# Keeping a weight conversion in its PSUM bank, in halves, and a last block with q in hp's bank and g rounded on ScalarE

## The chip, the cores and the metric

One Trainium2 chip, one of its cores. The metric is the device time of one execution in microseconds (us). TensorE does the matmuls, VectorE (DVE), ScalarE (ACT) and GpSimd (POOL) the elementwise work, SyncE (SP) issues the DMAs. The clock of TensorE that the profile shows as granted has two levels here, 1.2 and 2.4 GHz; a row's PEclk is its share of the higher one.

## The reference

Three layers over 3072 tokens of width 384, in float32: a linear attention with a decaying state, a layer with a curved activation, and a layer with a softmax-weighted linear unit and a normalization.

```python
for t in range(S):                      # 4 batches, 8 heads, 768 steps, head width 48
    cur = einsum('bhd,bhe->bhde', u * kt, vt)
    y[:, :, t] = einsum('bhd,bhde->bhe', rt, state + cur)
    state = wt[..., None] * state + einsum('bhd,bhe->bhde', kt, vt)
x = y as (3072, 384)
h = x @ w_in                            # 384 x 2048
x = (h - tanh(h)) @ w_out               # 2048 x 384
h = x @ w_in2                           # 384 x 1024
solu = h * softmax(h)
out = ((solu - mean) / sqrt(var + 1e-6) * g_ln) @ w_out2    # 1024 x 384
```

The weights arrive as 64-bit floats and are turned into pairs of 32-bit numbers on the chip.

## The kernel before, in words

**Stages.** The 24 units of attention (128 tokens each) feed six blocks of 512 tokens. A block has 16 steps m, one for each 128 columns of w_in. In a step `part1` makes `hp` (9 matmuls, one PSUM bank, pool `ps_h` with two buffers), then the activation is worked out in elementwise steps, and `part2`, two steps later in the program, adds 9 matmuls into the three banks `x2p`. Attention units 0 to 3 run first, the others between the steps. After the last block a second part with 24 tiles of 128 tokens does the third layer (`b_h`, `b_t`, `b_o`).

**The activation of a step** is a chain over engines: ACT squares `hp` into `t` (L339), DVE makes `y` from `hp` and `t` (L340), ACT makes a second square `p` from `t` (L342), DVE combines `p` and `y` (L344), ACT writes a range check into `q` (L345), and then `y` is rounded into `gs[:, 0]` (on ACT at L347 or on POOL at L349), and POOL writes the rest into `gs[:, 1]` (L350). In block 0 `p` is `hp` itself, in PSUM, and the rounding is on ACT; in blocks 1 to 5 `p` is `q`, in SBUF, and the rounding is on POOL.

**A conversion** (`convert`) takes 128 rows of 768 64-bit floats, half of w_in and half of w_out: `H_` are the upper words, `L_` the lower words, both with a stride of two words in the SBUF tile `raw`. ACT scales `L_` in place (L118). DVE shifts and masks `H_` into `a` (L125, the shift), joins the sign bits (L126, the or-step), and adds `L_` as an exact 32-bit integer (L127, the add; an instruction of its own that works on 16-bit elements, so 768 words are 1536 elements; the profile calls it CUSTOM_DVE_ANT_0 and the program's order ISA). Then ACT rounds into `hi` (L130) and POOL subtracts (L131).

- `conv_a` converts the first layer's weights into `wa`, 16 times, during the attention of units 0 to 3 and block 0. It passes `bank=ps_a`: `a` is a PSUM bank of the pool `ps_a`, which has three buffers and serves attention's transposes and products too.
- `conv_b` converts the second layer's weights into `wb`, 8 times, during the last block. It passes no bank, so `a` is the tile `cv_x` in SBUF, and the shift and the or-step are done in two halves of 384.

**What sets the order.** The program is recorded step by step (`fast_path`), and a scheduler then sets each engine's order. Engines run their own list in order, so an instruction that waits holds up those behind it. The tile `raw` has two buffers (pool `cvr`); the next load on SP's queue waits until the add has read `L_`.

Of the kernel before, what the change touches and what calls it, by code (L numbers as in the profile page):

```python
# [14 lines left out]
ALU = mybir.AluOpType  # L15
# [4 lines left out]
NT, DM, FF, FF2 = 3072, 384, 2048, 1024  # L20
# [5 lines left out]
NB = NT // BLK  # L26
# [29 lines left out]
class Kern:  # L56
# [52 lines left out]
    def convert(self, pool, raw, hi, lo, scale=None, bank=None):  # L109

        nc, v = self.nc, self.nc.vector
        flat = raw.rearrange("p i f two -> p (i f) two")
        H_, L_ = flat[:, :, 1], flat[:, :, 0]
        x = pool.tile([128, 2 * DM], U32, tag="cv_x", name="cv_x")
        xf = x.bitcast(F32)
        nc.scalar.activation(L_, L_, AF.Copy, scale=2.0**-29)  # L118
        for i in range(2):
            s = slice(i * DM, (i + 1) * DM)  # L120
            if bank is None:
                a = x[:, s]
            else:
                a = bank.tile([128, 4, C], F32, tag="a", name="cv_a").rearrange("p j t -> p (j t)")[:, 0:DM].bitcast(U32)
            v.tensor_scalar(a, H_[:, s], 3, 0x3FFFFFF8, ALU.logical_shift_left, ALU.bitwise_and)  # L125
            v.scalar_tensor_tensor(x[:, s], H_[:, s], 0xC0000000, a, ALU.bitwise_and, ALU.bitwise_or)  # L126
        v.tensor_tensor(x, x, L_, ALU.add)  # L127
        if scale is not None:
            nc.scalar.activation(xf[:, DM:], xf[:, DM:], AF.Copy, scale=scale)
        nc.scalar.copy(hi, xf)  # L130
        nc.gpsimd.tensor_tensor(lo, xf, hi, ALU.subtract)  # L131
# [196 lines left out]
    def part1(self, i, m):  # L328
        nc, v, g = self.nc, self.nc.vector, self.nc.gpsimd
        hp = self.ps_h.tile([128, BLK], F32, tag="h", name="hp")  # L330
        xs = self.xs[i % 2]
        seq = [(a, b, j) for j in range(KM) for a, b in ((1, 0), (0, 1), (0, 0))]
        for n, (a, b, j) in enumerate(seq):
            self.mm(hp, self.wa[:, a, m, j * 128:(j + 1) * 128], xs[:, b, j], start=n == 0, stop=n == len(seq) - 1)  # L334
        t = self.gp.tile([128, BLK], F32, tag="t", name="t")
        q = self.gp.tile([128, BLK], F32, tag="q", name="q")
        y = self.gp.tile([128, BLK], F32, tag="y", name="y")
        gs = self.gs.tile([128, 2, BLK], F32R, tag="g", name="g")
        nc.scalar.activation(t, hp, AF.Square)  # L339
        v.tensor_tensor(y, hp, t, ALU.mult)  # L340
        p = hp if i == 0 else q
        nc.scalar.activation(p, t, AF.Square, bias=self.c_fsb, scale=F_S)  # L342
        col = 2 * NU + i * NM + m
        v.scalar_tensor_tensor(y, p, F_E, y, ALU.add, ALU.mult)  # L344
        self.last_act = nc.scalar.activation(q, t, AF.Relu, bias=self.c_t2, accum_out=self.flags[:, col:col + 1])  # L345
        if i == 0:
            nc.scalar.copy(gs[:, 0], y)  # L347
        else:
            g.tensor_scalar(gs[:, 0], y, 1.0, 1.0, ALU.mult, ALU.mult)  # L349
        g.tensor_tensor(gs[:, 1], y, gs[:, 0], ALU.subtract)  # L350
        return gs
# [419 lines left out]
```

## Time and profile before

| | us |
|---|---|
| median of 3 runs | 837.1 (836.93 to 837.52) |
| the profiled execution's own time | 833.47 |
| its span, first to last instruction | 831.7 |
| PE busy in the span | 779.4 |
| DVE busy | 548.6 |
| ACT busy | 490.5 |
| POOL busy | 377.2 |

The span is what the trace covers; the execution's own time has 1.8 us around it. The busy time of PE is modelled, since matmuls are pipelined: where it is full, the interval from one matmul to the next tells more. Shares over the whole span mix stages with different limits, so they are read stage by stage.

### The profile page before, as it was taken

How to read it: one execution, taken by the hardware profiler on the slowest of the kernel's cores; microseconds unless marked ns; L12 is line 12 of the kernel's file. 1: busy time of each engine (PE TensorE's matmuls, PEld its weight loads, DVE VectorE, ACT ScalarE, POOL GpSimd, SP SyncE). 2: the span in 40 equal slices, each digit the busy share in tenths (PEclk: the TensorE clock that was granted, in tenths of full speed). 3: DMA queues.
4: the chain of work that ended last, by engine and by line, in shares of the span. 5: the costliest groups of instructions: out<-in, count | busy, mean ns of one | idle time of the engine just before them, and what ended most of it. 6: DMA issues, size and time to landing. Idle time of an engine off the chain costs nothing.

```text
span 831.7 us, 13450 instructions
## 1 busy us (share of the span) xinstructions
PE 779.4 (94%) x4706; PEld 649.1 (78%) x4706; DVE 548.6 (66%) x997; ACT 490.5 (59%) x928; POOL 377.2 (45%) x360
## 2 busy tenths in 40 slices
PE   3778988999999999999999999889989999999996
PEld 2656766778878888888888788667879999999996
DVE  4688889666664566565556763895287577667763
ACT  3436776677666767677677765655445454445442
POOL 3544765655555655556556465676412111111110
PEclk9988998899999999999999999999999999999998
DMA  9966567435455554463434220410021111111101
GB/s 164 166 107 127 138 146 151 136 100 115 90 120 114 125 108 105 107 157 81 119 100 130 82 81 25 140 50 2 10 67 39 48 39 48 39 48 39 48 29 33
DMA packets 151309, 74.32 MB, mean 89 GB/s; under 512 B 107328, under 2 KB 142784, under 8 KB 151232
## 3 DMA queue, kind: packets, MB, share of 16 engines
q1 hardware_dynamic: 151232, 73.37, 37.0%
q8 instruction: 39, 0.64, 0.3%
q14 instruction: 38, 0.31, 0.1%
HBM read 61.54 MB, written 9.44 MB: 85 GB/s over the span
## 4 chain that ended last, share of the span: by engine, by line
PE 75%; DVE 11%; DMA 4%; issue 2%; POOL 2%; ACT 2%; SPq 2%; DVEq 0%; ACTq 0%; POOLq 0%
PE hp L334 19%; PE x2p L357 18%; PE o L457 12%; PE h L412 11%; PE qk L254 3%; PE tp L218 3%; DVE cv_x L126 2%; PE tt L446 2%; DVE cv_x L127 2%; PE y L296 2%; PE y L293 2%; DMA raw<-in_moe_w_out_dram 1%; DVE cv_x L125 1%; DMA raw<-in_moe_w_in_dram 1%; PE kt L260 1%
## 5 line engine op out<-in xcount | busy, mean ns | idle before, releaser
L357 PE MATMUL x2p<-g,wa 128*128 128x512 f32 x864 | 226.4, 401 | 9.0 <-POOL g L350 4.6
L334 PE MATMUL hp<-xs,wa 128*128 128x512 f32 x864 | 225.8, 403 | 6.7 <-POOL wa L131 3.2
L334 PEld LDWEIGHTS hp<-xs,wa 128*128 128x128 f32 x864 | 162.5, 192 | 45.2 <-POOL wa L131 3.7
L357 PEld LDWEIGHTS x2p<-g,wa 128*128 128x128 f32 x864 | 160.3, 191 | 46.0 <-POOL g L350 6.3
L350 POOL TENSOR_TENSOR g<-y,g 128x512 fp32r<-128x512 f32 x96 | 129.3, 1347 | 17.4 <-ACT g L347 9.7
L340 DVE TENSOR_TENSOR y<-hp,t 128x512 f32<-128x512 f32 x96 | 66.2, 689 | 106.6 <-ACT t L339 103.6
L457 PE MATMUL o<-wb,ts 128*128 128x384 f32 x576 | 110.0, 341 | 1.0 <-DVE ts L448 1.0
L345 ACT ACTIVATE q<-t,cst 128x512 f32<-128x512 f32 x96 | 69.5, 724 | 68.1 <-DVE y L344 67.8
L412 PE MATMUL h<-wb,x2s 128*128 128x512 f32 x432 | 103.8, 392 | 2.8 <-DVE so L432 2.4
L349 POOL TENSOR_SCALAR g<-y 128x512 fp32r<-128x512 f32 x80 | 53.9, 674 | 114.8 <-DVE y L344 111.4
L457 PEld LDWEIGHTS o<-wb,ts 128*128 128x128 f32 x576 | 100.5, 188 | 2.9 <-DVE ts L448 1.3
L412 PEld LDWEIGHTS h<-wb,x2s 128*128 128x128 f32 x432 | 80.6, 188 | 19.8 <-issue 3.0
L339 ACT ACTIVATE t<-hp 128x512 f32<-128x512 f32 x96 | 56.6, 591 | 44.8 <-PE hp L334 44.6
L437 POOL TENSOR_TENSOR st<-st,cst 128x1 f32<-128x1 f32 x24 | 13.5, 563 | 136.2 <-DVE st L436 134.8
L344 DVE SCALAR_TENSOR_TENSOR y<-q,y 128x512 f32<-128x512 f32 x80 | 65.4, 818 | 10.6 <-ACT q L342 5.6
L342 ACT ACTIVATE q<-t,cst 128x512 f32<-128x512 f32 x80 | 57.7, 722 | 2.0
L435 ACT ACTIVATE e<-so 128x1024 f32<-128x1024 f32 x24 | 25.4, 1059 | 49.4 <-DVE so L434 49.4
L425 DVE TENSOR_REDUCE st<-h 128x1 f32<-128x1024 f32 x24 | 29.4, 1224 | 28.6 <-PE h L412 27.1
L428 DVE TENSOR_REDUCE part<-e 128x32 f32<-128x1024 f32 x24 | 29.3, 1220 | 27.9 <-ACT e L427 27.9
L218 PE MATMUL tp<-ident,rkw 128*128 128x128 f32 x264 | 41.9, 292 | 6.0 <-DMA rkw<-in_w_dram 5.7
L402 POOL TENSOR_TENSOR x2s<-x2s 128x384 fp32r<-128x384 f32 x24 | 24.4, 1018 | 48.3 <-ACT x2s L401 40.0
L131 POOL TENSOR_TENSOR wa<-cv_x,wa 128x768 fp32r<-128x768 f32 x16 | 29.4, 1838 | 35.3 <-ACT wa L130 35.3
(114 smaller groups left out, 1211.1 us busy)
## 6 DMA issues: line engine op xcount, KB each, us to landing
raw<-in_moe_w_out_dram SPq DMA_DIRECT2D x48, 384.0 KB, 4.0
raw<-in_moe_w_in_dram SPq DMA_DIRECT2D x64, 144.0 KB, 3.2
raw<-in_moe_w_in_dram SPq DMA_DIRECT2D x16, 384.0 KB, 3.1
rkw<-in_w_dram SPq DMA_DIRECT2D x24, 192.0 KB, 4.3
rkw<-in_r_dram SPq DMA_DIRECT2D x24, 192.0 KB, 4.5
rkw<-in_k_dram SPq DMA_DIRECT2D x24, 192.0 KB, 3.9
vt<-in_v_dram SPq DMA_DIRECT2D x24, 192.0 KB, 4.4
x2d<-x2o SPq DMA_DIRECT2D x18, 256.0 KB, 2.2
```

The lines of the kernel that those rows point to most:

```text
L218: self.nc.tensor.transpose(p[:, j], self.rkw[u % 2][:, i, 2 * j:2 * j + 2, :], self.ident)
L334: self.mm(hp, self.wa[:, a, m, j * 128:(j + 1) * 128], xs[:, b, j], start=n == 0, stop=n == len(seq) - 1)
L339: nc.scalar.activation(t, hp, AF.Square)
L340: v.tensor_tensor(y, hp, t, ALU.mult)
L342: nc.scalar.activation(p, t, AF.Square, bias=self.c_fsb, scale=F_S)
L344: v.scalar_tensor_tensor(y, p, F_E, y, ALU.add, ALU.mult)
L345: self.last_act = nc.scalar.activation(q, t, AF.Relu, bias=self.c_t2, accum_out=self.flags[:, col:col + 1])
L349: g.tensor_scalar(gs[:, 0], y, 1.0, 1.0, ALU.mult, ALU.mult)
L350: g.tensor_tensor(gs[:, 1], y, gs[:, 0], ALU.subtract)
L357: self.mm(self.x2p[d], self.wa[:, a, m, sl], gs[:, b], start=m == 0 and n == 0, stop=m == NM - 1 and n == 2)
L412: self.mm(p[:, f], xs[:, a, j], self.wb[:, b, 4 * f:4 * f + 4, j * 128:(j + 1) * 128], start=q == 0, stop=q == 8)
L457: self.mm(p, ts[:, a, k], self.wb[:, b, k, DM:], start=q == 0, stop=q == 3 * NM2 - 1)
```

## The change

In `convert` with a bank, the or-step writes back into the PSUM bank, and the add reads the bank and writes `x`, once for each half of 384 words. Without a bank (`conv_b`), the shift and the or-step are each one instruction over 768 words, in `x`, and the add stays one instruction. In the last block `p` is `hp`, and the rounding of `g` is on ACT, as in block 0.

```diff
@@ convert
-        for i in range(2):
-            s = slice(i * DM, (i + 1) * DM)
+        n = 1 if bank is None else 2
+        for i in range(n):
+            s = slice(i * 2 * DM // n, (i + 1) * 2 * DM // n)
             if bank is None:
-                a = x[:, s]
+                a = x
             else:
                 a = bank.tile([128, 4, C], F32, tag="a", name="cv_a").rearrange("p j t -> p (j t)")[:, 0:DM].bitcast(U32)
             v.tensor_scalar(a, H_[:, s], 3, 0x3FFFFFF8, ALU.logical_shift_left, ALU.bitwise_and)
-            v.scalar_tensor_tensor(x[:, s], H_[:, s], 0xC0000000, a, ALU.bitwise_and, ALU.bitwise_or)
-        v.tensor_tensor(x, x, L_, ALU.add)
+            v.scalar_tensor_tensor(a, H_[:, s], 0xC0000000, a, ALU.bitwise_and, ALU.bitwise_or)
+            v.tensor_tensor(x[:, s], a, L_[:, s], ALU.add)
@@ part1
-        p = hp if i == 0 else q
+        ends = i in (0, NB - 1)
+        p = hp if ends else q
@@
-        if i == 0:
+        if ends:
             nc.scalar.copy(gs[:, 0], y)
```

The lines of the changed kernel are numbered one higher from L120 on (the shift is L126, the or-step L127, the add L128) and two higher from L342 on (L342 is L344 there, L344 is L346, L350 is L352).

In block 0, DVE's list around the fifth conversion of `conv_a` (`cv_a` is the bank, `cv_x` the tile in SBUF, `xs` and `x` belong to attention). Before:

```order
L125 TENSOR_SCALAR cv_a<-raw 128x384
L344 SCALAR_TENSOR_TENSOR y<-hp,y 128x512
L125 TENSOR_SCALAR cv_a<-raw 128x384
L300 TENSOR_TENSOR xs_140<-y,xs_140 112x3x128
L301 TENSOR_TENSOR x_138<-y,x_138 112x128
L126 SCALAR_TENSOR_TENSOR cv_x<-raw,cv_a 128x384 x2
L125 TENSOR_SCALAR cv_a<-raw 128x384
L127 ISA cv_x<-raw,cv_x 128x1536
```

The same place in the changed kernel:

```order
L126 TENSOR_SCALAR cv_a<-raw 128x384
L301 TENSOR_TENSOR xs_140<-y,xs_140 112x3x128
L302 TENSOR_TENSOR x_138<-y,x_138 112x128
L126 TENSOR_SCALAR cv_a<-raw 128x384
L346 SCALAR_TENSOR_TENSOR y<-hp,y 128x512
L127 SCALAR_TENSOR_TENSOR cv_a<-raw,cv_a 128x384 x2
L341 TENSOR_TENSOR y<-hp,t 128x512
L128 ISA cv_x<-raw,cv_a 128x768 x2
```

The or-steps now write the bank, one add over 1536 elements has become two over 768 that read the bank, and an L341 stands between or-steps and adds, so both banks are held until after it.

At the start of the last block, DVE's list (`cv_x` and `raw` are those of `conv_b`). Before:

```order
L125 TENSOR_SCALAR cv_x<-raw 128x384 x2
L126 SCALAR_TENSOR_TENSOR cv_x<-raw,cv_x 128x384 x2
L340 TENSOR_TENSOR y<-hp,t 128x512
L127 ISA cv_x<-raw,cv_x 128x1536
L125 TENSOR_SCALAR cv_x<-raw 128x384 x2
L344 SCALAR_TENSOR_TENSOR y<-q,y 128x512
L340 TENSOR_TENSOR y<-hp,t 128x512
L126 SCALAR_TENSOR_TENSOR cv_x<-raw,cv_x 128x384 x2
L344 SCALAR_TENSOR_TENSOR y<-q,y 128x512
L127 ISA cv_x<-raw,cv_x 128x1536
```

The same place in the changed kernel:

```order
L126 TENSOR_SCALAR cv_x<-raw 128x768
L127 SCALAR_TENSOR_TENSOR cv_x<-raw,cv_x 128x768
L341 TENSOR_TENSOR y<-hp,t 128x512
L128 ISA cv_x<-raw,cv_x 128x1536
L126 TENSOR_SCALAR cv_x<-raw 128x768
L341 TENSOR_TENSOR y<-hp,t 128x512
L346 SCALAR_TENSOR_TENSOR y<-hp,y 128x512
L127 SCALAR_TENSOR_TENSOR cv_x<-raw,cv_x 128x768
L128 ISA cv_x<-raw,cv_x 128x1536
L346 SCALAR_TENSOR_TENSOR y<-hp,y 128x512
```

A conversion has three instructions in place of five, the combining step reads `hp`, and its place among the conversions hardly moves.

In the same stretch, POOL's list (`g` is `gs`). Before:

```order
L131 TENSOR_TENSOR wb<-cv_x,wb 128x768 x2
L349 TENSOR_SCALAR g<-y 128x512
L131 TENSOR_TENSOR wb<-cv_x,wb 128x768
L350 TENSOR_TENSOR g<-y,g 128x512
L349 TENSOR_SCALAR g<-y 128x512
L350 TENSOR_TENSOR g<-y,g 128x512
L131 TENSOR_TENSOR wb<-cv_x,wb 128x768
```

And in the changed kernel:

```order
L132 TENSOR_TENSOR wb<-cv_x,wb 128x768 x2
L352 TENSOR_TENSOR g<-y,g 128x512
L132 TENSOR_TENSOR wb<-cv_x,wb 128x768
L352 TENSOR_TENSOR g<-y,g 128x512
L132 TENSOR_TENSOR wb<-cv_x,wb 128x768
```

The roundings of `g` are gone from POOL; on ACT they now stand once a step, between the chain's other instructions and those of the conversions.

## Rows read from the trace of the kernel before

**Rows 1.** The page: span, busy time of each engine with its share.
```profile
span 831.7 us, 13450 instructions
PE 779.4 (94%) x4706; PEld 649.1 (78%) x4706; DVE 548.6 (66%) x997; ACT 490.5 (59%) x928; POOL 377.2 (45%) x360
```

**Rows 2.** Busy time by stretch (columns as the first line says; x counts instructions).
```profile
core 0: us, PE busy (x) PEld busy (x) DVE busy (x) ACT busy (x) POOL busy (x), PEclk, DMA share, GB/s
60.00:160.00 100.00, 87.22 (x501) 67.94 (x503) 87.52 (x152) 67.12 (x127) 59.53 (x41) 0.90 0.59 137
160.00:520.00 360.00, 359.46 (x2397) 292.80 (x2393) 215.42 (x384) 249.11 (x501) 205.59 (x196) 1.00 0.44 105
520.00:572.00 52.00, 45.03 (x180) 33.66 (x179) 44.53 (x48) 31.17 (x57) 34.20 (x27) 0.97 0.22 77
572.00:600.00 28.00, 28.00 (x125) 23.14 (x124) 10.02 (x15) 14.37 (x28) 14.29 (x15) 1.00 0.00 1
```

**Rows 3.** The chain that ended last, pieces on DVE (start us, us, what).
```profile
72.36 1.45 DVE cv_x L127
...
99.48 2.08 DVE cv_x L127
...
113.97 1.72 DVE cv_x L127
...
129.66 1.85 DVE cv_x L127
...
542.54 3.14 DVE cv_x L126 x2
```

**Rows 4.** Tile cv_x, 0 to 160 us (ns min/median/max, first and last start).
```profile
L126 DVE SCALAR_TENSOR_TENSOR cv_x<-raw,cv_a x32: 532/544/557, 16.5 to 157.6; 128x384 uint32<-128x384 uint32 x32
L127 DVE CUSTOM_DVE_ANT_0 cv_x<-raw,cv_x x16: 941/950/2143, 19.1 to 158.7; 128x1536 uint16<-128x1536 uint16 x16
```

**Rows 5.** DVE's instructions in order of time, block 0 (start us, us).
```profile
97.02 0.94 DVE L127 CUSTOM_DVE_ANT_0 cv_x<-raw,cv_x 128x1536 uint16<-128x1536 uint16 x1
97.88 0.67 DVE L344 SCALAR_TENSOR_TENSOR y<-hp,y 128x512 f32<-128x512 f32 x1
98.48 0.53 DVE L126 SCALAR_TENSOR_TENSOR cv_x<-raw,cv_a 128x384 uint32<-128x384 uint32 x1
98.94 0.54 DVE L203 TENSOR_REDUCE dg<-inv 128x8 f32<-128x384 f32 x1
```

**Rows 6.** Tile cv_x, 515 to 570 us.
```profile
L125 DVE TENSOR_SCALAR cv_x<-raw x12: 347/766/2006, 522.0 to 556.4; 128x384 uint32<-128x384 uint32 x12
L126 DVE SCALAR_TENSOR_TENSOR cv_x<-raw,cv_x x12: 545/810/2193, 524.1 to 559.3; 128x384 uint32<-128x384 uint32 x12
L127 DVE CUSTOM_DVE_ANT_0 cv_x<-raw,cv_x x6: 944/952/2389, 525.7 to 561.6; 128x1536 uint16<-128x1536 uint16 x6
```

**Rows 7.** DVE's groups, 521 to 571 us (busy us, mean ns, idle before).
```profile
L126 DVE SCALAR_TENSOR_TENSOR cv_x<-raw,cv_x 128x384 uint32<-128x384 uint32 x12 | 13.2, 1136 | 0.0
L125 DVE TENSOR_SCALAR cv_x<-raw 128x384 uint32<-128x384 uint32 x12 | 10.5, 912 | 4.0 <-POOL wb L131 4.0
L344 DVE SCALAR_TENSOR_TENSOR y<-q,y 128x512 f32<-128x512 f32 x9 | 9.5, 1053 | 1.0 <-ACT q L342 0.6
L127 DVE CUSTOM_DVE_ANT_0 cv_x<-raw,cv_x 128x1536 uint16<-128x1536 uint16 x6 | 7.1, 1190 | 0.4
L340 DVE TENSOR_TENSOR y<-hp,t 128x512 f32<-128x512 f32 x9 | 6.2, 684 | 2.9 <-ACT t L339 2.1 <-POOL g L349 0.8
```

**Rows 8.** POOL's rounding of g, 521 to 571 us.
```profile
L349 POOL TENSOR_SCALAR g<-y 128x512 fp32r<-128x512 f32 x9 | 6.8, 753 | 11.8 <-DVE y L344 11.8
```

**Rows 9.** Groups by form, whole span: block 0's forms.
```profile
L342 ACT ACTIVATE hp<-t,cst 128x512 f32<-128x512 f32 x16 | 11.0, 687 | 2.9 <-DVE y L340 2.9
L344 DVE SCALAR_TENSOR_TENSOR y<-hp,y 128x512 f32<-128x512 f32 x16 | 10.9, 683 | 1.0 <-ACT hp L342 0.9
L347 ACT CAST g<-y 128x512 fp32r<-128x512 f32 x16 | 9.8, 615 | 2.5 <-DVE y L344 2.4
```

**Rows 10.** All engines in order of time, last block.
```profile
549.49 0.69 DVE L340 TENSOR_TENSOR y<-hp,t 128x512 f32<-128x512 f32 x1 [0.69 <-ACT t L339]
...
554.25 0.68 DVE L344 SCALAR_TENSOR_TENSOR y<-q,y 128x512 f32<-128x512 f32 x1
```

**Rows 11.** What PE waited for, 60 to 165 us (us in total, times, longest).
```profile
PE hp L334 <- DVE y L344: 2.7, 1, 2.7
```

## The prediction

> **What bounds the kernel now.** The page comes first: PE is busy for 94% of the span [rows 1], which says little, since the change touches stages that differ. So the busy time by stretch comes next [rows 2]. Three kinds of stretch are to be seen. From 160 to 520 us PE is full (359.5 of 360) and DVE at 215.4 of 360, 60%: nothing that the change does to DVE, ACT or POOL is worth anything there. From 60 to 160 us (attention's first units, block 0 and the `conv_a` conversions) DVE is at 87.5% and PE is idle for 12.8 us. From 520 to 572 us (most of the last block, the `conv_b` conversions) DVE is at 44.5 of 52, 86%, and PE is not full. From 572 to 600 us the conversions are over, and PE is full again, with one matmul every 28.0 / 125 = 0.224 us.
>
> The last number says what 520 to 572 loses. Its 180 matmuls need 180 x 0.224 = 40.3 us, so 52 - 40.3 = 11.7 us are lost there, and no change to the elementwise work can win more than that in this stretch. The chain that ended last agrees on who is to blame: in both stretches it runs through the conversions on DVE [rows 3].
>
> Why do those take long? The tile's view answers. In 0 to 160 us the or-step, which reads one operand from PSUM, takes 532 to 557 ns in all 32 instances; the add, which reads both from SBUF, takes 941 ns at best and 2143 at worst [rows 4]. In the last block, where all three instructions have their operands in SBUF, all three spread: 347 to 2006, 545 to 2193, 944 to 2389 ns [rows 6]. DVE's instructions with their tensors in SBUF stretch, here beside POOL that is 60 to 66% busy [rows 2], and the ones with a PSUM operand do not.
>
> **The change, part A: `conv_a`.** The add's tail goes. Of the 16 adds five are disturbed, four of them on the chain: 1.45, 2.08, 1.72 and 1.85 us [rows 3] against 0.95, together 3.3 us too long; the fifth stands off it. Against this stand 16 more instructions. One instruction is followed by the next before its own end: an add of 0.94 us begins 0.86 us ahead of the next instruction, an or-step of 0.53 us 0.46 us ahead [rows 5]. If an add over 768 elements costs what the or-step over 384 words costs, 0.46 us (both halve 0.86 to 0.43 and pay some fixed part again), two cost 0.92 against 0.86: 16 x 0.06 = 1.0 us more. The gain on the chain is 3.3 - 1.0 = 2.3 us; I take 2.5, since POOL's own instructions are less held up too. The shift is as before. The or-step now writes PSUM, for which there is no row on DVE with PSUM on both sides. From below: the same kind of square on ACT takes 687 ns into PSUM [rows 9], and nothing on DVE suggests a gain. From above: if reading and writing took turns at the bank, each of its 384 elements would cost 1.05 ns more (0.684 us for 512 elements against 0.545 for 384 [rows 6, 7]), 0.4 us x 32 = 13 us. I take no change, being nearest to the or-step's own 545 ns [rows 4].
>
> Each bank is held through the adds instead of the or-step, about 1.5 us longer with the instructions that stand between. There are three buffers, and attention waits on DVE for longer than that anyway in this stage; I charge nothing, and 2 us if that cover is missing.
>
> **Part B: the last block.** Its 30 conversion instructions in this stretch take 13.2 + 10.5 + 7.1 = 30.8 us [rows 7]. Undisturbed they would take 12 x 0.347 + 12 x 0.545 + 6 x 0.944 = 16.4 us [rows 6]. So 14.4 us are waits, 0.48 us an instruction. Afterwards there are 18. Widths of 768 have no row. The or-step: 0.545 + 384 x 1.05 ns = 0.95 us. The shift: at 0.347 for 384 it runs at about twice that pace, so 0.347 + 0.20 = 0.55 us (at most twice 0.347, 0.69). With the add at 0.944 a conversion needs 2.45 us, six 14.7 us. The waits scale with the number of instructions and with POOL's share. POOL loses 6.8 us of rounding [rows 8]: 34.2 - 6.8 = 27.4, over a stretch of 45 us 61% against 66%. So 18 x 0.48 x 61/66 = 8.0 us. Sum 22.7 against 30.8: DVE saves 8.1 us. The combining step takes 1.053 us with its operands in SBUF [rows 7] and 0.683 with `hp` [rows 9]: 9 x 0.37 = 3.3 us. DVE falls from 44.5 to 33.1 us, below the 40.3 that PE needs.
>
> ACT takes over nine roundings of 0.615 us, and its second square becomes 0.03 us cheaper: 31.2 + 5.5 - 0.3 = 36.4 us. In a stretch of 45 us that is 81%, the highest of the elementwise engines; DVE would be at 74%. So not all of the 11.7 us comes back. For the size I use the two stretches that are known: PE loses nothing at a DVE share of 60% and 12.8% at 87.5%; in between, at 74%, 6.5% of 45 us or 3 us, and somewhat more for ACT. I take 4.7 lost and 7 us won.
>
> `hp` is held until the combining step, not just until L340. With two buffers a step may keep its bank for two steps less its own filling. At PE's pace a step is 18 matmuls, 4.0 us, so 8.1 - 2.0 = 6.0 us; t and y take 1.3 us of it, and 4.7 us are left for p and the combining step. The worst case here starts L340 at 549.49 and ends L344 at 554.93, 4.8 us after L340 [rows 10]; the usual one is far shorter. In block 0, which has this form already, PE waited on L344 once, for 2.7 us [rows 11]. So: hidden, and some 3 us if not.
>
> **The sum.** 2.5 + 7 = 9.5 us. Span 831.7 - 9.5 = 822.2; own time 833.47 - 9.5 = 824.0. The profiled execution is 3.6 us below the median of the runs shown, so the median becomes 837.1 - 9.5 = 827.6 us.
>
> **The rivals.**
>
> *The add from PSUM runs at half pace (slower).* Now 1536 elements of 16 bits pass in 0.86 us, two of them in the 1.05 ns that other instructions need for one element. If an operand in PSUM allows only one, a half of 768 elements costs some 0.46 + 384 x 1.05 ns = 0.86 us, two 1.72 instead of 0.86, and 16 x 0.86 = 13.8 us come into a stage where DVE is nearly full, less the 3.3 of the waits: +10.5. With part B at 7 us the sum is +3.5: 840.6 us. It decides from a half of (16 x 0.86 + 3.3 + 7) / 32 = 0.75 us upwards. For it: no row has a 16-bit operand in PSUM. Against it: the 32-bit instructions of DVE show no price for PSUM, 545 ns with it and 545 without [rows 4, 6]. The Trainium skill speaks on both sides. VectorE: DVE Perf Modes, section "The perf-mode tier table (the rule you actually need)", lists an operation on two tensors at its single pace as soon as any operand is in PSUM; by that rule this rival holds. Vector Engine (DVE) Microarchitecture Reference, section "Performance modes — why throughput varies by op and dtype", asks for the double pace on two sources only that all operands have 2 bytes and step one, and wants SBUF just for the mode that uses both ports on one source; by that the forecast holds. No run here shows either yet.
>
> *The last block's wait moves to `hp` and ACT.* PE waits for the combining step behind two wide conversion instructions, now up to 1 us each undisturbed, and ACT at 81% is late with p. Part B then gives back nothing: 837.1 - 2.5 = 834.6 us. For it: the combining steps of the first two steps stand behind conversion instructions in DVE's new order. Against it: [rows 11].
>
> *The wide instructions wait just as long, and the start gains nothing.* If a wait depends on the time that DVE spends in SBUF, not on the number of instructions, the 14.4 us shrink only by POOL's share, to some 13; part B is 1.7 + 1.4 + 3.3 us on DVE, worth 4, and part A is hidden behind the loads of `raw`: 833 us.
>
> **How the numbers follow.** Forecast 0.56; half pace 0.24; wait on `hp` and ACT 0.12; waits unchanged 0.08. A measurement of this kernel tells about 0.2%, 1.7 us, from no change. Faster: nearly all of the forecast (0.53), most of the second (0.09) and third rival (0.07), a little of the first (0.03), 0.72. Slower: three quarters of the first, 0.18, and 0.02 of others, 0.20. The same: 0.08. The forecast's own range is 823 (all of the 11.7 and 2.5 us) to 833; with the half pace on the other side the range is 822 to 841.
>
> **What would show it.** The add's halves at about 0.55 us each without spread mean that part A is right; 0.95 us means the first rival. The or-step into PSUM should stay at 0.55. In the last block the step interval should be near 4.1 us soon, the combining step 0.68 without spread, POOL without roundings, and PE's waits should not name L346. The prediction is wrong if the or-step in PSUM doubles, if PE waits for attention's banks in the first 160 us, or if the new order moves work in the full stretch, which should keep its 360 us.

## The result and the profile after

The changed kernel takes 823.5 us (median of 4 runs, 822.77 to 823.97) where the kernel before takes 837.3 us beside it (836.93 to 837.66): a ratio of 0.9835 with an interval of 0.9818 to 0.9852, 13.8 us less. The forecast was 827.6 us. The profiled execution of the changed kernel took 822.77 us, and its page begins so [rows 1]:

```profile
span 821.0 us, 13437 instructions
PE 769.9 (94%) x4706; PEld 643.2 (78%) x4706; DVE 528.6 (64%) x997; ACT 499.1 (61%) x944; POOL 364.9 (44%) x344
```

The two spans differ by 10.7 us (831.7 and 821.0), 3 us less than the times: the profiled execution of the kernel before, 833.47, lies below all four of its timed runs. In the later sets that kernel takes 834.4 to 834.6 us, and the two parts of the change, run alone there, win 8.5 and 2.8 us, so the size is nearer to 11 us than to 13.8. To see where these come from I set marks in both timelines: the start of the first square `t` of a step, the first reduction of the third layer, and the end. The changed kernel is ahead of the one before by:

| mark | before, us | after, us | ahead by |
|---|---|---|---|
| block 0, first step | 71.8 | 73.2 | -1.4 |
| block 1, first step | 175.1 | 165.1 | 10.0 |
| block 2, ninth step | 303.0 | 295.7 | 7.3 |
| last block, first step | 523.1 | 515.3 | 7.8 |
| last block, last step | 594.8 | 586.2 | 8.6 |
| first reduction of the third layer | 603.4 | 592.9 | 10.5 |
| end | 831.7 | 821.0 | 10.7 |

So on these two traces the start gives 7.8 us and the last block 2.7, where the prediction had 2.5 and 7. The sum came out, its two terms did not.

**The start.** The tile's view of `cv_a` in the changed kernel, 0 to 170 us (ns min/median/max):

```profile
L126 DVE TENSOR_SCALAR cv_a<-raw x32: 542/554/568, 15.8 to 152.4; 128x384 uint32<-128x384 uint32 x32
L127 DVE SCALAR_TENSOR_TENSOR cv_a<-raw,cv_a x32: 544/556/564, 16.4 to 154.1; 128x384 uint32<-128x384 uint32 x32
L128 DVE CUSTOM_DVE_ANT_0 cv_x<-raw,cv_a x32: 528/547/561, 18.4 to 154.7; 128x768 uint16<-128x768 uint16 x32
```

The add over 768 elements of 16 bits, one operand in PSUM, takes 547 ns and never more than 561; the or-step that reads and writes the same bank takes 556, against 544 into SBUF [rows 4]. Both prices that were left open are settled: none.

The busy time by stretch, with the columns of [rows 2]:

```profile
60.00:160.00 100.00, 90.94 (x560) 69.63 (x557) 86.71 (x175) 70.90 (x135) 61.81 (x45) 0.96 0.64 142
160.00:520.00 360.00, 358.24 (x2377) 292.79 (x2375) 214.13 (x379) 249.17 (x503) 205.60 (x195) 1.00 0.43 103
512.00:562.00 50.00, 43.18 (x184) 33.63 (x183) 33.66 (x36) 36.29 (x67) 30.22 (x19) 1.00 0.25 83
562.00:590.00 28.00, 28.00 (x125) 23.02 (x123) 10.01 (x15) 18.63 (x35) 7.94 (x7) 1.00 0.01 1
```

DVE is as full in the first stretch as before (86.7 of 100), yet PE does 560 matmuls there instead of 501. The column to look at is PEclk: 0.96 against 0.90. More closely, the same stretches in the kernel before:

```profile
112.00:115.00 3.00, 1.40 (x4) 1.12 (x5) 3.00 (x5) 2.16 (x5) 2.83 (x2) 0.81 1.12 222
135.00:140.00 5.00, 2.63 (x11) 1.80 (x10) 4.97 (x7) 4.22 (x9) 2.79 (x2) 1.00 0.45 77
140.00:145.00 5.00, 4.46 (x16) 3.39 (x15) 4.61 (x9) 2.93 (x8) 1.92 (x2) 0.62 1.00 224
145.00:150.00 5.00, 5.00 (x16) 3.74 (x15) 2.54 (x5) 3.44 (x6) 4.81 (x4) 0.50 0.60 175
```

and in the changed one:

```profile
135.00:140.00 5.00, 4.20 (x19) 2.64 (x18) 4.42 (x9) 3.40 (x7) 4.13 (x3) 1.00 0.87 192
...
145.00:150.00 5.00, 4.74 (x32) 3.20 (x31) 4.96 (x11) 4.05 (x7) 2.17 (x2) 1.00 0.53 132
```

In the kernel before, PE is idle for 2.4 of the 5 us from 135, and then its granted clock falls: 0.62, and 0.50 from 145 to 150, which is the lower level, 1.2 GHz, all the time. Its timeline (start us, us) shows what that does to the nine products of a step:

```profile
134.72 2.35 PE L334 MATMUL hp<-xs,wa 128*128 128x512 f32 x9
139.43 0.96 PE L357 MATMUL x2p<-g,wa 128*128 128x512 f32 x3 [2.37 <-ACT g L347]
...
142.69 4.21 PE L334 MATMUL hp<-xs,wa 128*128 128x512 f32 x9
```

2.35 us before the wait, 4.21 after it. In the changed kernel the clock stays at 1.00. Over 71.8 to 175 us (both kernels, one window each) the clock is 0.93 before and 1.00 after, which is 103.2 x 0.07 = 7.2 us of full clock (the shares are rounded), and PE's idle time is 10.0 us before and 6.2 after, 3.9 us less. Together that is 11.1 us; between the first two marks the changed kernel gains 11.4. Some 2.7 us are given back until block 2, where PE is full in both kernels: the changed order leaves products of the steps for later (434 matmuls of `hp` and `x2p` between these two marks, against 418).

**The last block.** The conversions' tile, 510 to 562 us [rows 6], and DVE's groups, 512 to 562 us [rows 7]:

```profile
L126 DVE TENSOR_SCALAR cv_x<-raw x6: 545/558/2189, 514.2 to 543.3; 128x768 uint32<-128x768 uint32 x6
L127 DVE SCALAR_TENSOR_TENSOR cv_x<-raw,cv_x x6: 943/959/2490, 516.4 to 543.9; 128x768 uint32<-128x768 uint32 x6
L128 DVE CUSTOM_DVE_ANT_0 cv_x<-raw,cv_x x6: 948/1238/2377, 517.9 to 546.0; 128x1536 uint16<-128x1536 uint16 x6
```

```profile
L128 DVE CUSTOM_DVE_ANT_0 cv_x<-raw,cv_x 128x1536 uint16<-128x1536 uint16 x6 | 8.7, 1458 | 0.2
L127 DVE SCALAR_TENSOR_TENSOR cv_x<-raw,cv_x 128x768 uint32<-128x768 uint32 x6 | 8.2, 1374 | 0.1
L341 DVE TENSOR_TENSOR y<-hp,t 128x512 f32<-128x512 f32 x9 | 6.2, 684 | 3.9 <-ACT t L340 2.7 <-POOL g L352 1.2
L346 DVE SCALAR_TENSOR_TENSOR y<-hp,y 128x512 f32<-128x512 f32 x9 | 6.2, 684 | 4.0 <-ACT hp L344 4.0
L126 DVE TENSOR_SCALAR cv_x<-raw 128x768 uint32<-128x768 uint32 x6 | 6.0, 1007 | 6.4 <-POOL wb L132 6.4
```

The conversions take 8.7 + 8.2 + 6.0 = 22.9 us of DVE, forecast 22.7; the combining step takes 0.684 without spread. DVE's work was forecast well. What PE waited for in that stretch was not:

```profile
PE hp L335 <- DVE y L346: 6.5, 4, 2.4
```

PE waits for the bank `hp` until the combining step has read it. The timeline of all engines shows why (start us, us):

```profile
536.42 0.69 DVE L341 TENSOR_TENSOR y<-hp,t 128x512 f32<-128x512 f32 x1 [1.11 <-ACT t L340]
...
537.05 1.64 DVE L126 TENSOR_SCALAR cv_x<-raw 128x768 uint32<-128x768 uint32 x1
...
538.33 2.07 POOL L132 TENSOR_TENSOR wb<-cv_x,wb 128x768 fp32r<-128x768 f32 x1
538.72 2.49 DVE L127 SCALAR_TENSOR_TENSOR cv_x<-raw,cv_x 128x768 uint32<-128x768 uint32 x1
541.25 0.96 DVE L128 CUSTOM_DVE_ANT_0 cv_x<-raw,cv_x 128x1536 uint16<-128x1536 uint16 x1
542.12 0.68 DVE L346 SCALAR_TENSOR_TENSOR y<-hp,y 128x512 f32<-128x512 f32 x1
...
542.86 2.34 PE L335 MATMUL hp<-xs,wa 128*128 128x512 f32 x9 [1.96 <-DVE y L346]
...
543.59 1.44 POOL L352 TENSOR_TENSOR g<-y,g 128x512 fp32r<-128x512 f32 x1 [3.19 <-issue]
543.91 1.94 DVE L127 SCALAR_TENSOR_TENSOR cv_x<-raw,cv_x 128x768 uint32<-128x768 uint32 x1
544.99 2.56 POOL L132 TENSOR_TENSOR wb<-cv_x,wb 128x768 fp32r<-128x768 f32 x1
...
545.98 2.38 DVE L128 CUSTOM_DVE_ANT_0 cv_x<-raw,cv_x 128x1536 uint16<-128x1536 uint16 x1
```

Between y (L341) and the combining step (L346) of this step stands a whole conversion, three instructions that run from 537.05 to 542.21, with L126 and L127 held up beside POOL (1.64 and 2.49 us, at best 0.55 and 0.94). From the end of L341 at 537.11 to the end of L346 at 542.80 are 5.7 us; the prediction had 4.7 us of cover for p and the combining step. PE starts 0.06 us after L346's end.

### The profile page after: what moved, and what is told of

Its sections match the earlier page's. It is cut to its first block, busy times and chain, and to the rows that moved or that the text cites. A ratio compares the mean times of both kernels' runs of the same rounds, so it can differ in the third digit from the quotient of the medians.

```text
span 821.0 us, 13437 instructions
## 1 busy us (share of the span) xinstructions
PE 769.9 (94%) x4706; PEld 643.2 (78%) x4706; DVE 528.6 (64%) x997; ACT 499.1 (61%) x944; POOL 364.9 (44%) x344
## 4 chain that ended last, share of the span: by engine, by line
PE 76%; DVE 7%; DMA 5%; ACT 4%; SPq 3%; issue 3%; POOL 2%; DVEq 0%; ACTq 0%; POOLq 0%
PE hp L335 19%; PE x2p L359 19%; PE o L459 12%; PE h L414 11%; PE tp L219 3%; DMA raw<-in_moe_w_out_dram 3%; PE tt L448 2%; PE qk L255 2%; PE y L294 2%; PE y L297 2%; DMA raw<-in_moe_w_in_dram 1%; SPq L315 1%; PE kt L261 1%; DVE cv_x L128 1%; SPq L305 1%
## 5 line engine op out<-in xcount | busy, mean ns | idle before, releaser
L335 PE MATMUL hp<-xs,wa 128*128 128x512 f32 x864 | 222.9, 399 | 11.2 <-DVE y L346 7.5
L359 PE MATMUL x2p<-g,wa 128*128 128x512 f32 x864 | 223.3, 397 | 1.6 <-POOL g L352 1.1
L359 PEld LDWEIGHTS x2p<-g,wa 128*128 128x128 f32 x864 | 158.2, 188 | 37.7 <-POOL g L352 3.7
L352 POOL TENSOR_TENSOR g<-y,g 128x512 fp32r<-128x512 f32 x96 | 126.0, 1312 | 57.6 <-ACT g L349 38.9
L341 DVE TENSOR_TENSOR y<-hp,t 128x512 f32<-128x512 f32 x96 | 66.2, 689 | 106.6 <-ACT t L340 103.3
L347 ACT ACTIVATE q<-t,cst 128x512 f32<-128x512 f32 x96 | 69.5, 724 | 57.8 <-DVE y L346 57.3
L351 POOL TENSOR_SCALAR g<-y 128x512 fp32r<-128x512 f32 x64 | 43.8, 684 | 86.7 <-DVE y L346 78.6
L439 POOL TENSOR_TENSOR st<-st,cst 128x1 f32<-128x1 f32 x24 | 13.8, 576 | 134.1 <-DVE st L438 124.4
L346 DVE SCALAR_TENSOR_TENSOR y<-q,y 128x512 f32<-128x512 f32 x64 | 51.8, 809 | 7.8 <-ACT q L344 4.0
L437 ACT ACTIVATE e<-so 128x1024 f32<-128x1024 f32 x24 | 25.4, 1060 | 50.9 <-DVE so L436 49.0
L344 ACT ACTIVATE q<-t,cst 128x512 f32<-128x512 f32 x64 | 46.3, 723 | 1.8
L429 ACT ACTIVATE e<-h,st 128x1024 f32<-128x1024 f32 x24 | 26.8, 1118 | 32.0 <-DVE st L428 31.1
```

What stands on the lines that cost most here:

```text
L359: self.mm(self.x2p[d], self.wa[:, a, m, sl], gs[:, b], start=m == 0 and n == 0, stop=m == NM - 1 and n == 2)
```

## The experiments

Theory 1, as the runs are told here: DVE's instructions with both sources in SBUF, and the shift within SBUF, wait while POOL works, and a source in PSUM (for the shift the destination) frees them; PE loses time where such waits stand ahead of something that it needs. The rivals, one for each pair of runs, put the gain down to the order that comes with the halves, to the work that is moved between the engines, or hold a wait for hidden. All were timed in five rounds, in three sets, each set on one chip beside the kernel before (medians 834.4, 834.6 and 834.5 us in the sets). The expectations of experiments 1 to 3 count from the 837 us of the section above, so their sizes are to be compared, not their times.

**1. The `conv_a` edit alone** (against the kernel before; the last block is as it was).

```diff
-            v.scalar_tensor_tensor(x[:, s], H_[:, s], 0xC0000000, a, ALU.bitwise_and, ALU.bitwise_or)
-        v.tensor_tensor(x, x, L_, ALU.add)
+            v.scalar_tensor_tensor(a, H_[:, s], 0xC0000000, a, ALU.bitwise_and, ALU.bitwise_or)
+            if bank is not None:
+                v.tensor_tensor(x[:, s], a, L_[:, s], ALU.add)
+        if bank is None:
+            v.tensor_tensor(x, x, L_, ALU.add)
```

> Only the first layer's conversions are changed (or-step back into the bank, add read from the bank in halves); the last block is as before. Theory 1 (the start wins because the adds no longer wait in SBUF): the halves take 0.55 us without spread, the trace of this kernel is 7 us ahead of before at step 40 and stays so to the end, 827 to 831 us by the clock of timed runs. Rival (the 7 us of the changed kernel came from the new order and TensorE's clock, not from this edit): the start is ahead by at most 3 us, 834 us or more.

825.3 us, ratio 0.9898 (0.9873 to 0.9923): 8.5 us less in the times, 8.2 us on the trace at every mark from block 2 to the last block. The granted clock over 71.8 to 175 us is 1.00. The adds take 526 to 556 ns, without spread, as theory 1 had it. The start alone gives some 8 us, three times its term in the sum.

**2. The last-block edits alone** (the `conv_b` part of `convert`, `p = hp` and the rounding on ACT; `conv_a` as before).

> The first layer's conversions are as before; conv_b's shift and or-step over 768, and the last block with hp and g's rounding on ScalarE, are changed. Theory 1: the start is as before, the last block wins about 3 us net, because matmuls wait for hp behind the combining step for some 6 us; 833 to 835 us. The prediction's own size for this part was 7 us: 830 us. Rival (the last block's edits only look useful beside the shorter start): no gain, 836 to 838 us.

831.7 us, ratio 0.9966 (0.995 to 0.9982): 2.8 us less. From the last block's first square to the first reduction it takes 77.5 us (603.6 - 526.1), as the changed kernel does (592.9 - 515.3 = 77.6), against 80.3 before. This block length repeats well: experiment 3 and experiment 1, which don't touch the last block, have 80.3. The start repeats less well: here it is 3.3 us later than before at block 1, and up to block 5 each engine's order is the same as before's. PE waited 6.0 us for `hp` behind L346, three times. Theory 1's size and its waits came out (3 and 6 us), the prediction's 7 us did not.

**3. Halves, but the or-step still writes SBUF** (against before; the add is done in halves on two SBUF operands, so that the counts are those of experiment 1 without its operand in PSUM; the order that the scheduler makes is another from DVE's 102nd instruction on, at 68 us).

```diff
-        v.tensor_tensor(x, x, L_, ALU.add)
+            if bank is not None:
+                v.tensor_tensor(x[:, s], x[:, s], L_[:, s], ALU.add)
+        if bank is None:
+            v.tensor_tensor(x, x, L_, ALU.add)
```

> Before, with one thing different: the first layer's add is in halves, but the or-step still writes SBUF, so each half has both operands in SBUF. Theory 1: the halves still wait for GpSimd, some of them over 1 us, 16 more instructions; the same as before or up to 2 us slower, 836 to 840 us. Rival (the halves or the new order make the gain): ahead by 5 us or more at step 40, 832 us or less.

833.8 us, ratio 0.9986 (0.9971 to 1.0). Its adds:

```profile
L128 DVE CUSTOM_DVE_ANT_0 cv_x<-raw,cv_x x32: 542/550/2683, 18.3 to 161.6; 128x768 uint16<-128x768 uint16 x32
```

The median is that of the add from PSUM, but single ones reach 2683 ns. The clock sags as in the kernel before (0.98, 0.88 and 0.91 over 72 to 118, 118 to 145 and 145 to 175 us). So the halves alone don't win the start. For the operand in PSUM speaks that its adds don't spread (experiment 1), but another order comes with it, and no run kept the operand and its order apart.

**4. The changed kernel with p in q in the last block** (SBUF; the rest of the change stays).

```diff
-        p = hp if ends else q
+        p = hp if i == 0 else q
```

> The changed kernel, with p of the last block in q in SBUF again; g's rounding stays on ScalarE and the conversions are as changed. Theory 1 (hp held until the combining step costs what part B was short of): matmuls no longer wait for that step, the combining step waits for GpSimd again (0.8 us or more in the mean); if the hold is dearer than the waits, 819 to 823 us; if the waits are dearer, 824 to 828 us. Rival (the hold costs nothing net): 823.5 us plus 3 us for the combining step's waits, 826 us or more.

823.3 us, ratio 0.9861 (0.9839 to 0.9884), which can't be told from the changed kernel's 0.9835 (0.9818 to 0.9852). The medians and the ratios differ on which is faster, so the times decide nothing between the expectation's cases. The block takes 76.6 us, 0.9 less, so by it the hold is dearer than the waits, by little. DVE works longer (the combining step 15.9 us for 16, against 11.0), and PE no longer waits behind L346, but for y and POOL:

```profile
PE hp L335 <- DVE y L341: 3.8, 3, 3.0
PE x2p L359 <- POOL g L352: 1.8, 2, 1.4
```

What `hp` saves on DVE, its hold costs on PE.

**5 to 7. The parts of the last block, each on top of the `conv_a` edit.** Number 5 fuses the shift and the or-step of `conv_b` (p in q, rounding on POOL); 6 has the rounding on ACT (halves, p in q); 7 the rounding on ACT and p in `hp` (halves).

Number 5, against the changed kernel:

```diff
-        ends = i in (0, NB - 1)
+        ends = i == 0
```

Number 6, against experiment 1:

```diff
-        if i == 0:
+        if i in (0, NB - 1):
             nc.scalar.copy(gs[:, 0], y)
```

Number 7, against number 6:

```diff
-        p = hp if i == 0 else q
+        p = hp if i in (0, NB - 1) else q
```

> The conv_a edit, and conv_b with the shift and the or-step fused to 768 words; in the last block p stays in q and the rounding on POOL. Theory 1 (a DVE instruction with both operands in SBUF waits once, whatever its length, while POOL works): 3 instructions instead of 5 in a conversion save some 12 x 0.48 us less POOL's share on DVE, of which PE gets back a part: 1 to 2 us below the kernel with the conv_a edit alone (825.3), so 823.5 to 824.5. Rival (the waits grow with the time spent in SBUF): the two agree within 0.5 us.

> The conv_a edit, and in the last block the rounding of g on ScalarE; p stays in q, conv_b keeps its halves. Theory 1 (POOL's work is what DVE's instructions wait for): nine roundings less on POOL shorten the waits of the 30 conversion instructions, and g comes earlier: 2 to 3 us below the conv_a edit alone, 822.5 to 823.5. Rival (the DVE waits in the last block are hidden behind the products that TensorE has in stock): within 0.5 us of it.

> As the one with the rounding on ScalarE, and p in hp's bank too; conv_b keeps its halves. Theory 1 with the wait on hp: DVE saves some 3 us on the combining step, but TensorE waits for hp behind it for some 6 us in the block, so it is 0 to 1 us slower than with p in q. Rival (the hold of hp is hidden, as the prediction said): 2 to 3 us faster than with p in q.

Number 5: 823.0 us, ratio 0.9868 (0.9848 to 0.9889). Number 6: 826.5 us, 0.9902 (0.9885 to 0.9918). Number 7: 824.6 us, 0.9888 (0.987 to 0.9906). Against experiment 1 (0.9898), the fusing gives some 2 us (the block 77.8 us against 80.3), the rounding on ACT nothing, and `hp` on top of it 1.9 us in the medians, all with intervals that overlap. Theory 1's time for 5 nearly came out, but not its reason: at one wait for each instruction the fusing should have saved DVE some 12 x 0.48 = 5.8 us of waits, and the conversions fell from 30.8 to 27.0 us, of which 1.8 us is work and 2.0 waits. The instructions are fewer and wait longer, the adds 2.1 us in the mean (517 to 594.8 us):

```profile
L128 DVE CUSTOM_DVE_ANT_0 cv_x<-raw,cv_x 128x1536 uint16<-128x1536 uint16 x6 | 12.7, 2118 | 0.4
L127 DVE SCALAR_TENSOR_TENSOR cv_x<-raw,cv_x 128x768 uint32<-128x768 uint32 x6 | 7.4, 1232 | 0.1
L126 DVE TENSOR_SCALAR cv_x<-raw 128x768 uint32<-128x768 uint32 x6 | 6.9, 1148 | 5.1 <-POOL wb L132 5.1
```

Theory 1's expectation for 6 was wrong: the roundings taken off POOL cut the conversions' time on DVE from 30.8 to 25.4 us, yet PE got none of it. For 7, theory 1 had it at 0 to 1 us slower than 6 and the rival at 2 to 3 us faster; it came 1.9 us faster in the times and in the block's length, so the rival was nearer. PE waits for `hp` behind the combining step there too, but once, 2.9 us, and not four times: how often the hold bites depends on the order.

**8. `conv_b` through a PSUM bank too.** The kernel of experiment 4, and `conv_b` passes a bank of the pool that the second part uses later, so it runs in halves as `conv_a` does.

```diff
-        self.convert(pool, raw, self.wb[:, 0, k], self.wb[:, 1, k], self.gl[:, k:k + 1])
+        self.convert(pool, raw, self.wb[:, 0, k], self.wb[:, 1, k], self.gl[:, k:k + 1],
+                     bank=lambda: self.ps_r.tile([128, DM], F32, tag="o", name="cv_a"))
```

> The changed kernel with p in q in the last block, and conv_b through a PSUM bank as well (one bank of the pool that the second part uses), in halves. Theory 1: the or-step and the add have an operand in PSUM and don't spread any more, 0.55 us each; the six conversions of the last block cost DVE some 17 us instead of 22.9, and the end comes 2 to 3 us earlier than with conv_b in SBUF (823.2), some 820.5 us. Rival (with one bank, shift, or-step and add of a half follow one another without anything between, and DVE's waits were not what TensorE waited for): the same or slower than 823.2.

816.3 us, ratio 0.9793 (0.9774 to 0.9811): 7 us below experiment 4 (823.3, 0.9861), on which it is built, more than twice what theory 1 expected. Below the changed kernel it is 7.2 us in the times and 3.5 in the ratios, since that one was timed beside 837.3 us. The tile's view, 510 to 560 us:

```profile
L128 DVE CUSTOM_DVE_ANT_0 cv_x<-raw,cv_a x15: 539/553/556, 510.4 to 549.9; 128x768 uint16<-128x768 uint16 x15
L126 DVE TENSOR_SCALAR cv_a<-raw x14: 548/561/562, 511.4 to 546.5; 128x384 uint32<-128x384 uint32 x14
L127 DVE SCALAR_TENSOR_TENSOR cv_a<-raw,cv_a x14: 547/561/564, 512.0 to 547.1; 128x384 uint32<-128x384 uint32 x14
```

Not one instruction of a conversion waits. DVE gains less by that than was expected: the eleven halves in the block take 18.2 us, so the twelve of six conversions some 19.9, against 22.8 in experiment 4 and the 17 of the expectation. The shift pays for its way into PSUM, 0.56 us for 384 words where within SBUF 0.347 is its least [rows 6]. Yet PE got back nearly all of its idle time, 5.7 us against 0.9. The bank and the halves come together here; halves in SBUF alone, with the add among them, were not run for `conv_b`. The middle of the block is worth a look:

```profile
520.00:550.00 30.00, 29.12 (x127) 23.40 (x126) 27.14 (x45) 27.23 (x52) 19.07 (x12) 1.00 0.39 132
```

DVE is at 90% and ACT at 91%, and PE lacks only 0.9 us of 30.

**9. As 8, with p in `hp`** in the last block, as the change has it.

> The kernel with conv_b through a PSUM bank (816.3), and in the last block p in hp's bank as the change has it. Theory 1: no DVE instruction of the last block is longer than 0.7 us any more and TensorE is full there (68.4 of 69.3 us), so neither the combining step's shorter time nor hp's hold is worth anything: within 1 us of 816.3, and no wait of TensorE on the combining step over 1 us. Rival (the hold itself costs, whatever stands ahead of the combining step): TensorE waits on it for 4 us or more, 818 to 820.

819.2 us, ratio 0.9808 (0.9783 to 0.9833); the block takes 72.2 us against 69.3 in experiment 8. Theory 1 was wrong, the rival right about the time, though the wait is under its 4 us:

```profile
521.61 1.84 PE L335 MATMUL hp<-xs,wa 128*128 128x512 f32 x4 [2.67 <-DVE y L346]
```

There is one wait, at the block's second step, 2.67 us, and over the 5 us from 522 the granted clock is 0.67. The hold costs this even where no instruction on DVE is longer than 0.7 us. Here ACT is late:

```profile
515.11 0.90 ACT L118 ACTIVATE raw<-raw 128x768 uint32<-128x768 uint32 x1 [2.34 <-DMA raw<-in_moe_w_out_dram]
517.28 1.08 ACT L340 ACTIVATE t<-hp 128x512 f32<-128x512 f32 x2
520.13 0.69 ACT L344 ACTIVATE hp<-t,cst 128x512 f32<-128x512 f32 x1
```

The square t stands in ACT's list behind a conversion's scaling, which waits 2.34 us for the transfer of `raw`, and p (L344) starts at 520.13, 0.9 us after both y are done (519.19). The bank is free at 521.55, and PE goes on at 521.61.

**10. As 8, with the rounding of g on POOL** (`ends = i == 0`), so that of the change's last-block edits none is left.

> The kernel with conv_b through a PSUM bank (816.3), and in the last block the rounding on POOL as before the change, p in q: so nothing of the change's last-block edits but the conversion's bank. Theory 1 (DVE's waits behind POOL were the whole loss): within 1 us of 816.3, with the conversion's three instructions still at 0.55 us. Rival (POOL's nine roundings and the later g count by themselves): TensorE waits on POOL's subtraction, 817.5 to 819.

814.3 us, ratio 0.9754 (0.9732 to 0.9777): the fastest of all, 20 us below the kernel before and some 9 below the changed one (7 in the ratios). Neither expectation had this. Against experiment 8 it is 2 us, with intervals that just touch, and 1.4 us of the block. Its last block:

```profile
515.00:582.90 67.90, 67.83 (x298) 55.07 (x296) 42.92 (x67) 46.73 (x88) 44.77 (x40) 1.00 0.20 67
```

PE is full, with POOL at 44.8 of 67.9 us: POOL's roundings harm nothing when DVE's conversions don't wait for POOL. The combining step, with p in q, still does (0.99 us in the mean against 0.68), and PE is full all the same.

**11. POOL's subtraction left out in the last block** (the kernel of experiment 4; the products read the rounded part twice).

```diff
-        g.tensor_tensor(gs[:, 1], y, gs[:, 0], ALU.subtract)
+        if i < NB - 1:
+            g.tensor_tensor(gs[:, 1], y, gs[:, 0], ALU.subtract)
```

> The changed kernel with p in q in the last block (823.2) and conv_b in SBUF, and in the last block POOL's subtraction (the rest of g) is left out; the products that would read the rest read the rounded part instead, so the number of products is the same. Theory 1 (it is POOL's work that DVE's instructions with two SBUF operands wait for): the six conversions of the last block take DVE 15 to 17 us instead of 22.8, with no instruction beyond 1.2 us except where POOL subtracts in wb, and TensorE loses little: 815 to 819. Rival (the transfers or ScalarE make DVE's instructions spread): they still take over 20 us and still reach 2 us.

816.2 us, ratio 0.9778 (0.9754 to 0.9801); the block takes 71.1 us. The conversions take 4.9 + 9.1 + 5.7 = 19.7 us on DVE, between the 15 to 17 of theory 1 and the 20 of the rival, so the total does not decide, and the time doesn't either, since PE's waits for POOL (1.8 us in experiment 4) go as well; the single instructions do. All six adds take 946 to 959 ns, in the changed kernel 948 to 2377. What is still long stands beside the one thing that POOL still does, the subtraction in `wb`:

```profile
530.86 0.55 DVE L126 TENSOR_SCALAR cv_x<-raw 128x768 uint32<-128x768 uint32 x1
531.40 1.85 POOL L132 TENSOR_TENSOR wb<-cv_x,wb 128x768 fp32r<-128x768 f32 x1 [1.61 <-ACT wb L131]
531.44 2.63 DVE L127 SCALAR_TENSOR_TENSOR cv_x<-raw,cv_x 128x768 uint32<-128x768 uint32 x1
534.20 0.96 DVE L128 CUSTOM_DVE_ANT_0 cv_x<-raw,cv_x 128x1536 uint16<-128x1536 uint16 x1
```

The or-step ends at 534.07, 0.82 us after POOL's instruction (533.25). In the changed kernel's timeline above, L127 ends 541.21, 0.81 after POOL's L132 (540.40), the next L127 at 545.85, 0.82 after L352 (545.03), and L128 at 548.36, 0.81 after L132 (547.55). So these instructions do not share time with POOL's: they wait for the end of the one that is running, and then run.

**The last block in one table.** Length from its first square to the first reduction, PE's idle time and granted clock in it, and DVE's time in the conversions, all from one window each, whose ends lie within 0.1 us of the marks (of the twelve halves of `conv_b`'s six conversions, eleven lie in the windows of 8, 9 and 10):

| kernel | length, us | PE idle, us | clock | conversions, us |
|---|---|---|---|---|
| before | 80.2 | 7.0 | 0.98 | 30.8 |
| 6: rounding on ACT | 80.2 | 6.5 | 0.96 | 25.4 |
| 7: rounding on ACT, `hp` | 78.3 | 4.7 | 0.96 | 24.9 |
| 5: fused | 77.8 | 7.3 | 1.00 | 27.0 |
| changed kernel | 77.5 | 6.8 | 1.00 | 22.9 |
| 4: fused, rounding on ACT | 76.6 | 5.7 | 1.00 | 22.8 |
| 9: bank, rounding on ACT, `hp` | 72.2 | 2.7 | 0.98 | 17.8 |
| 11: as 4, less POOL work | 71.1 | 0.8 | 1.00 | 19.7 |
| 8: bank, rounding on ACT | 69.3 | 0.9 | 1.00 | 18.2 |
| 10: bank | 67.9 | 0.1 | 1.00 | 18.2 |

PE is idle for as long in the changed kernel as before, 6.8 and 7.0 us. Most of its 2.7 us is clock: 0.98 over 80 us is 1.6 us. In experiment 5 it is the same: PE idle for 7.3 us, and the clock at 1.00.

## Why the prediction came out, and where its steps failed

The time, 823.5, lies 4.1 us below the forecast and inside the range. It is right in the sum and wrong in the split, and that is luck: part A gave 6 us more than its term and part B 4 us less.

- **"2.3 us; I take 2.5" for `conv_a`: mis-sized, it measured 8.5 us (experiment 1).** The mechanism was right as far as the runs go: the add with an operand in PSUM keeps its 547 ns, and experiment 3, without that operand (and in another order), loses the gain. The step priced only the excess of four adds on the chain. It left out what the stalls do to PE afterwards: after them its clock is at the lower level, and the change gives back 7.2 us of full clock in this stage against 3.9 us of idle time. [Rows 2] had it: PEclk 0.90 in that stretch, where the text read only the busy columns. The share of the clock is read from windows of two traces; no run kept the stalls and the clock apart.
- **"Half pace" (the rival at 0.24): refuted.** 547 ns, far from the 0.75 us at which it would decide. Of the pages of the Trainium skill, the section "The perf-mode tier table (the rule you actually need)" of VectorE: DVE Perf Modes does not hold for this instruction: by it a half would take the 0.95 us that the prediction names as this rival's sign, and it takes 0.55. The Trainium skill's Vector Engine (DVE) Microarchitecture Reference, section "Performance modes — why throughput varies by op and dtype", agrees with the trace.
- **"I take no change" for the or-step in PSUM: right**, 556 against 544 ns.
- **"I charge nothing" for the longer hold of the banks: right within 1 us**; PE waits once in the stage for a bank that an add was still reading, 0.7 us.
- **"DVE saves 8.1 us": right in the number**, the conversions take 22.9 us, forecast 22.7, and the combining step 0.684. Undisturbed, by the minima of the tile's view, six conversions would take 6 x (0.545 + 0.943 + 0.948) = 14.6 us; the other 8.3 are waits, forecast 8.0, by a rule that does not hold (below). The 1.05 ns an element come out as 1.09 by the two rows beside them, 0.139 us over 128 elements, which moves no instruction by more than 0.02 us.
- **"hidden, and some 3 us if not" for the hold of `hp`: the step that failed.** It was not hidden: 6.5 us of PE's waits, in four pieces. It allowed 4.7 us for p and the combining step and took the longest case of before, 4.8, for a rare one; with a conversion of three wide instructions between, 5.7 and 5.6 us are seen, and waits of 1.96 and 1.77 us. It also allowed 1.3 us for t and y. The longest wait, at the block's start, comes from there: y is done 2.7 us after the start of t (515.3 to 518.0), since it stands behind a shift that waits, and the combining step at 520.54:

```profile
514.22 2.19 DVE L126 TENSOR_SCALAR cv_x<-raw 128x768 uint32<-128x768 uint32 x1 [4.00 <-POOL wb L132]
...
520.59 2.33 PE L335 MATMUL hp<-xs,wa 128*128 128x512 f32 x9 [2.35 <-DVE y L346]
```

What the hold costs in the end differs by pair: the block is 2.9 us longer by it from experiment 8 to 9, as the named price has it, 0.9 from experiment 4 to the changed kernel, and 1.9 shorter from 6 to 7. The second rival had described this wait, and held [rows 11] against it, where block 0 shows it once for 2.7 us: one instance in 16 steps was evidence for it. It also had ACT late with p, which experiment 9 shows, beside a late t.
- **"PE loses nothing at a DVE share of 60% and 12.8% at 87.5%; in between, at 74%": the step that mis-sized part B**, 7 us forecast, 2.8 measured (experiment 2). In the changed kernel DVE is at 33.66 of 50 us, 67%, and PE loses 6.8; in the middle of experiment 8 DVE is at 90% and PE loses 0.9 of 30. The share does not tell. What fits these runs is how late the instruction comes that PE waits for: in the timeline above 5.2 us of conversion stand ahead of the combining step, and from the start of t to the end of y it is up to 7.2 us in experiment 4 and up to 3.6 in experiment 8, where the least is 1.3. That is read from the traces; no run varies it alone.
- **"The waits scale with the number of instructions and with POOL's share": wrong, and its size (8.0 against 8.3) was luck.** The runs that change one factor show it. With 18 instructions and the rounding still on POOL (experiment 5; POOL at 39.5 of 50 us from 514, 79%) the rule gives 18 x 0.48 x 79/66 = 10.3 us, and 27.0 - 14.6 = 12.4 are measured; with 30 and the rounding on ACT (6; 29.6 of 50, 59%) it gives 12.9, and 25.4 - 16.4 = 9.0 are measured. So POOL's roundings cost more than the rule has it, and the number of instructions counts for less. What the single instructions show: a wait lasts until the end of POOL's running instruction (experiment 11), and there is none when one source is in PSUM (8).
- **"The wide instructions wait just as long, and the start gains nothing" (third rival): refuted** for the start by experiment 1, and its 13 us of waits by the 8.3. Its rule, that the waits go with the time spent in SBUF, is not refuted by experiment 5: it gives 14.4 x 14.6/16.4 = 12.8 us there, and 12.4 are measured.

What stays open: why the start moves by 3 us between executions of an unchanged order (experiment 2), whether the start is won by the operand or by the order that comes with it, and whether `hp` or q is better beside the wide SBUF conversions, since the times of the changed kernel and of experiment 4 can't be told apart.

## What to carry to other kernels

Where VectorE and GpSimd work side by side, look at the spread of an instruction rather than its median: if its minimum is that of an undisturbed one and its maximum lies a GpSimd instruction higher, moving one of its two sources to PSUM takes the wait away, and the runs that did so won more here (7 us in the last block, 8 in the start) than any saving of VectorE's work. Price a stall of TensorE with what the granted clock does behind it, since in the start that column gave back nearly twice what the idle time did. Before a PSUM bank is held longer, count in each engine's order what stands between its first reader and its last, with their longest times and not their shortest.

## What the runs showed of the hardware

- An instruction of VectorE with both sources in SBUF that meets a running GpSimd instruction ends 0.81 to 0.82 us after that one's end (four instances shown, 0.96 us when undisturbed). The Trainium skill says so too: SBUF — State Buffer, section "SBUF: two separate sides", has whichever of the two starts first hold the shared ports for its whole instruction. These runs agree, and the same is seen from the other side: GpSimd's subtraction of 1.85 us takes 2.56 at 544.99. The shift within SBUF, with one source, waits as well: at 537.05 it ends 0.43 us after L352 on POOL (536.98 to 538.26), and undisturbed it takes 0.55. So each of the five ends as if it had begun 0.12 to 0.15 us ahead of GpSimd's end.
- The add, an operation on two tensors of 16-bit elements, goes at 547 ns for 768 elements with one source in PSUM and 550 with both in SBUF (experiments 1 and 3): PSUM costs it no pace. The shift does pay: 0.56 us for 384 words from SBUF into a bank (experiment 8), 0.347 at best within SBUF [rows 6].
- VectorE reads and writes one PSUM bank in one instruction at 556 ns for 384 elements of 32 bits, against 544 into SBUF.
- After an idle time of 2.67 us at the start of the last block in experiment 9, TensorE's granted clock was 0.67 over the 5 us from 522; after the 1.96 us at 542.86 in the changed kernel it stayed at 1.00 (512 to 562 us).
